# A transformer block on one core: the scale columns start from ones, one tile takes its scale from PSUM, the scale rows come in one block, the last transposes move ahead, and the second fc1 pass begins in other banks

## The chip, the cores and the metric

The kernel runs on one core of a Trainium2 chip. The core has five engines that each work through their own list of instructions in order: TensorE (PE, matrix products into the accumulator memory PSUM), VectorE (DVE), ScalarE (ACT), GpSimd (POOL) and SyncE (SP, which here only issues loads and stores). They wait for one another through semaphores. Transfers run on 16 DMA engines. PSUM has eight banks of 128 partitions by 512 float32 values. The metric is the device time of one execution in microseconds (us), the median of several runs.

## What is computed

A diffusion transformer block with modulation from a condition vector `c`, in bfloat16. There are B = 2 batches of N = 256 tokens, D = 1152 channels, F = 4608 hidden channels and two heads.

```python
mod = (_silu(c) @ w_mod).reshape(B, 6, 1, D)
shift_a, scale_a, gate_a, shift_m, scale_m, gate_m = [mod[:, i] for i in range(6)]
h = _layernorm(x, axis=-1) * (1 + scale_a) + shift_a
qkv = (h @ wqkv).reshape(B, N, 3, H, Dh)
...
attn = _softmax(jnp.einsum('bqhd,bkhd->bhqk', q, k) * Dh ** (-0.5), axis=-1)
a = jnp.einsum('bhqk,bkhd->bqhd', attn, v).reshape(B, N, D) @ wo
x = x + gate_a * a
h2 = _layernorm(x, axis=-1) * (1 + scale_m) + shift_m
m = _gelu(h2 @ w_fc1) @ w_fc2
return x + gate_m * m
```

The change touches the first layer norm with its scale `1 + scale_a`, the first projection that uses it (K), and the first product of the MLP (`h2 @ w_fc1`).

## The kernel before

**Planner.** The program text records every operation with its operands. A planner (class `Sched`) derives the dependencies and fixes each engine's order before anything runs. PE and SP keep the order in which the text records their work; DVE and ACT begin with the lists in `S.first` (L944) and then follow the planner's priorities; POOL follows the priorities. For PSUM the dependencies go by whole banks: an engine that reads a bank waits for the last matmul that PE wrote there, and PE waits for all readers before it writes the bank again. Nearly all matmuls are recorded by one helper line (L693) and the transposes on PE by another (L696), so in the profile they are told apart by form and by time.

**Tiles.** The 512 tokens are four tiles of 128: tiles 0 and 1 are batch 0, tiles 2 and 3 batch 1. The 1152 channels are nine groups of 128 (`KT = 9`); the first five (`KC = 5`) and the last four get their scale in two different ways.

**First layer norm** (L756). Tiles 1 and 3 take their statistics from DVE (L741, L742), tiles 0 and 2 from two ACT passes (L749, L750). POOL makes the reciprocal deviation (L745, L754). `xn_t` (L763, DVE) normalises the tile. `xn_T(t)` transposes it on PE in nine pieces into PSUM: for batch 0 into banks 4, 5 and 6, for batch 1 into 6, 4 and (group 8) 7.

**Scale, first five groups** (`sca`, `mod_kt`). Column-wise: for each group of the condition, five matmuls with two columns each add to ten columns of bank 7. The first one clears the bank. `sc1a` (L809, DVE) adds 1 and writes the ten columns to SBUF as `SC1A`. `hk` (L819 on DVE, L817 on ACT) multiplies a transposed piece by its column of `SC1A` and writes `HK`, the moving operand of the K product. `hk_0_0`, of group 0 and batch 0, reads the piece from SBUF; for the other four groups it is read from PSUM.

**K, first five groups** (L865). For batch 0, groups 0 to 4 are worked off one by one, each with four pairs of output columns (`k_pair`, two matmuls of 256 columns per pair). `xn_T(2)` stands behind group 1, `xn_T(3)` behind the first two pairs of group 4, then pairs 2 and 3 of group 4. The K product of batch 1 follows: `k_pair((0, 2, 1, 4, 3), 0, 1)`, which needs the five `hk` of batch 1.

**Scale, last four groups** (`scb`, L879). Row-wise: `quad_mm` makes for each of the nine groups of the condition four matmuls that use a quarter of the array each, into 32-partition stripes of bank 7. They stand in two blocks: condition groups 0 to 5, then six K matmuls of `k_pair((0, 2, 1), 1, 1)`, then condition groups 6 to 8. DVE then transposes the rows into columns (L888, `scb_T`), adds 1 (L890), and makes the `hk` of groups 5 to 8 (first of them `hk_5_0`), which K groups 5 to 8 need.

**Loads.** SP issues them in a fixed order from the start: x, the scale weights of the first five groups (in four pieces), K weights 0 to 4, the scale weights of the last four groups in three pieces of three condition groups each (`ld_sc5_0`, `ld_sc5_3`, `ld_sc5_6`), K weights 5 to 8, the shift weights, and then the Q weights, which overwrite the scale weights piece by piece and so wait for PE to have read them.

**MLP.** `xn2_T(t)` transposes the second norm's tiles 0 to 3 into PSUM (tile 2 into banks 7 and 6, tile 3 into banks 1 and 0: groups 0 to 3 in the first, 4 to 8 in the second). DVE (L1154) and ACT (L1157) scale and shift them into `H2T`. `fc1_tile(f, tok0, n)` (L1160) makes one 128-row piece of the hidden layer in one accumulator bank, which ACT empties with GELU (L1167). The accumulators rotate over the list `acc`: banks 2 to 5 at first. The first nine pieces (`F0 = 9`) are made for batch 0, then for batch 1; at that point (L1229) two banks are put at the front of the list:

```python
k = acc_rr[0] % 4
acc[:] = [0, 1] + acc[k:] + acc[:k]
```

So `fc1_0_256`, the first piece of batch 1, goes to bank 0 and `fc1_1_256` to bank 1. All later products take the six banks in turn.

Of the kernel before, what the change touches and what calls it, by code (L numbers as in the profile page):

```python
# [493 lines left out]
ALU = mybir.AluOpType  # L494
ACTF = mybir.ActivationFunctionType
# [5 lines left out]
KT = 9  # L501
# [8 lines left out]
KC = 5  # L510
# [5 lines left out]
def c_mm(n):  # L516
    return max(n / 2.4 + 2.5, 27.0)


def c_act(n, aps=0):  # L520
    return 190.0 + 0.8 * n + 75.0 * aps
# [10 lines left out]
def c_dve_fast(n):  # L532
    return 160.0 + 0.37 * n
# [10 lines left out]
def build_kernel(nc, x, c, wqkv, wo, w_mod, w_fc1, w_fc2, out):  # L544
    S = Sched()
# [4 lines left out]
    with (  # L550
# [4 lines left out]
        def sb(off, nbytes, dt=BF16):  # L555
            assert off % 4 == 0 and off + nbytes <= ARENA_BYTES, (off, nbytes)
            v = arena[:, off // 2:(off + nbytes) // 2]
            if dt == F32:
                v = v.bitcast(F32)
            return v  # L560

        def ps32(bank, c0=0, n=512):
            return psum[:, bank * 512 + c0: bank * 512 + c0 + n]

        def ps16(bank, c0=0, n=1024):
            v = psum[:, bank * 512: (bank + 1) * 512].bitcast(BF16)
            return v[:, c0:c0 + n]
# [15 lines left out]
        def misc(nbytes):  # L583
            o = mo[0]
            mo[0] += (nbytes + 3) // 4 * 4
            assert mo[0] <= ARENA_BYTES
            return o

        def wmat(o, f):
            return sb(o, KT * f * 2).rearrange("p (k f) -> p k f", k=KT)  # L590

        WSC = wmat(O_A, D)
# [41 lines left out]
        ONES = sb(misc(256), 256)  # L634
# [3 lines left out]
        ST = sb(misc(36), 36)  # L638
# [12 lines left out]
        NMR = sb(misc(16), 16, F32)  # L651
# [25 lines left out]
        def dve(cost, fn, reads, writes, name):  # L677
            return S.op("dve", cost, fn, reads=reads, writes=writes, name=name)

        def act(cost, fn, reads, writes, name):  # L680
            return S.op("act", cost, fn, reads=reads, writes=writes, name=name)
# [10 lines left out]
        def mm(o, l, r, st, sp, **kw):  # L692
            S.instr(lambda e: e.matmul(o, lhsT=l, rhs=r, start=st, stop=sp, **kw), reads=[l, r], writes=[o])  # L693
# [62 lines left out]
        for t in range(4):  # L756
            xt, xn, mv, rs = X[:, t, :], XN[:, t, :], MV[:, t, :], RSTD[:, t:t + 1]
            if t % 2 == 1:
                ln_stats_dve(xt, [X[:, t, i * CH:(i + 1) * CH] for i in range(NCH)], BN[:, t, :], mv, rs, "ln1_%d" % t)
            else:  # L760
                ln_stats_act(xt, xn, mv, SUMS[:, t:t + 1], rs, "ln1_%d" % t)
            m = MV[:, t, 0:1]
            dve(c_dve_fast(D), lambda e, xt=xt, xn=xn, m=m, rs=rs: e.tensor_scalar(out=xn, in0=xt, scalar1=m, scalar2=rs,  # L763
                                                                                 op0=ALU.subtract, op1=ALU.mult),
                [xt, m, rs], [xn], "xn_%d" % t)


        def xt_ps(b, kt, n=1):
            if b == 0:
                return (4, 5, 6)[kt // 4], (kt % 4) * 256  # L770
            return (7, 0) if kt == 8 else ((6, 4)[kt % 2], kt // 2 * 256)
# [8 lines left out]
        def xn_T_copy(b, kts, eng):  # L780
            bank, c0 = xt_ps(b, kts[0])
            n = len(kts)
            src = ps16(bank, c0, n * 256).rearrange("p (k t) -> p k t", k=n)
            st = kts[1] - kts[0] if n > 1 else 1
            copy_on(eng, HX[:, kts[0]:kts[-1] + 1:st, b * 256:(b + 1) * 256], src, n * 256, True, "xnT_cp%d_%d" % (b, kts[0]))

        def warm(n, tag):
            for i in range(n):
                S.unit("pe", 215.0, "warm_%s_%d" % (tag, i))
                mm(ps32(2), IDENT, Q4B, True, True)  # L790

        def mod_kt(W, kt, col0, name, fs=(0, 9)):
            S.unit("pe", (fs[1] - fs[0]) * 27.0, name)
            for f in range(*fs):
                mm(ps32(7, col0 + f * 2, 2), W[:, kt, f * 128:(f + 1) * 128], ST[:, kt:18:9], kt == 0 and f == fs[0], kt == KT - 1,
                   skip_group_check=True)

        def quads(w, g0, g1, q):
            return w.rearrange("p (g q c) -> p g q c", q=4, c=32)[:, g0:g1, q, :]

        def quad_mm(bank, w, g0, g1, kt):
            n = 32 * (g1 - g0)
            for q in range(4):
                o = psum[32 * q:32 * q + 2, bank * 512:bank * 512 + n].rearrange("p (g c) -> p g c", c=32)
                mm(o, ST[:, kt:18:9], quads(w, g0, g1, q), kt == 0, kt == KT - 1, tile_position=(0, 32 * q))

        def sc1a(ka, kb):
            m, o = ps32(7, 2 * ka, 2 * (kb - ka)), SC1A[:, 2 * ka:2 * kb]
            dve(170, lambda e: e.tensor_scalar(out=o, in0=m, scalar1=1.0, scalar2=None, op0=ALU.add), [m], [o], "sc1a_%d" % ka)  # L809


        def hk(kt, b, eng="dve"):
            dst, s1 = HK[:, kt, b * 256:(b + 1) * 256], SC1A[:, kt * 2 + b:kt * 2 + b + 1]
            bank, c0 = xt_ps(b, kt)
            src = ps16(bank, c0, 256) if kt < KC and kt + b > 0 else HX[:, kt, b * 256:(b + 1) * 256]
            if eng == "act":
                act(c_act(256, 1), lambda e: e.activation(out=dst, in_=src, func=ACTF.Copy, scale=s1), [src, s1], [dst], "hk_%d_%d" % (kt, b))  # L817
                return
            dve(256 if kt < KC else 200, lambda e: e.tensor_scalar(out=dst, in0=src, scalar1=s1, scalar2=None, op0=ALU.mult),  # L819
                [src, s1], [dst], "hk_%d_%d" % (kt, b))  # L820
# [10 lines left out]
        def k_pair(kts, i, b, bank=None):  # L831
            S.unit("pe", 2 * len(kts) * c_mm(256), "k%d_%d_%d" % (b, i, kts[0]))
            bank = KB[b][i] if bank is None else bank
            if kts[0] == 0:
                for kt in kts:
                    for half in range(2):
                        k_mm((kt,), 2 * i + half, b, bank, half)
            else:
                for half in range(2):
                    k_mm(kts, 2 * i + half, b, bank, half)  # L840
            if kts[-1] == KT - 1:
                eng = "act" if ev_rr[0] % 2 == 0 else "dve"
                ev_rr[0] += 1
                copy_on(eng, QK[:, 9 + 2 * i:11 + 2 * i, b * 256:(b + 1) * 256], ps32(bank).rearrange("p (j t) -> p j t", j=2), 512, False,
                        "k_ev%d_%d" % (b, i))

        warm(5, "b")
        for kt in range(0, 2):
            mod_kt(WSC, kt, 0, "sca_%d" % kt, (0, KC))
        warm(4, "c")  # L850
# [6 lines left out]
            mod_kt(WSC, kt, 0, "sca_%d" % kt, (0, KC))  # L857
        warm(1, "e")
        xn_T_copy(0, (0,), "dve")
        sc1a(0, KC)  # L860
        for kt in range(KC):
            hk(kt, 0, "act" if kt == 4 else "dve")
        xn_T_copy(0, (8,), "act")
        xn_T_copy(0, (5, 6, 7), "act")
        for kt in range(KC):  # L865
            for i in range(2 if kt == KC - 1 else 4):
                k_pair((kt,), i, 0)
            if kt == 1:
                xn_T(2)
        xn_T(3)  # L870
        k_pair((KC - 1,), 2, 0)
        k_pair((KC - 1,), 3, 0)
        xn_T_copy(1, (8,), "act")
        xn_T_copy(1, (5, 7), "act")
        xn_T_copy(1, (6,), "dve")
        for kt in range(KC):
            hk(kt, 1, "act" if kt % 2 else "dve")
        k_pair((0, 2, 1, 4, 3), 0, 1)
        S.unit("pe", 6 * 4 * 27.0, "scb_0")  # L879
        for kt in range(6):  # L880
            quad_mm(7, WSC[:, kt, :], KC, KT, kt)
        k_pair((0, 2, 1), 1, 1)
        S.unit("pe", 3 * 4 * 27.0, "scb_1")
        for kt in range(6, KT):
            quad_mm(7, WSC[:, kt, :], KC, KT, kt)
        n = 32 * (KT - KC)
        sct, scr = ps32(7, 0, n), MT[:, 0:n]
# [42 lines left out]
        for kt in range(KT):  # L930
            for b in range(2):
# [5 lines left out]
                else:  # L937
# [5 lines left out]

        S.first = {  # L944
# [5 lines left out]
        }  # L950

# [160 lines left out]
        acc = [2, 3, 4, 5]  # L1112
# [113 lines left out]
        dma(WFC2[:, 27:36, :], wfc2_v[:, 27:36, :], 9 * P * D * 2, "ld_wfc2_3", run=2304)  # L1226
        mlp_gate(last_h2T[0])
        k = acc_rr[0] % 4
        acc[:] = [0, 1] + acc[k:] + acc[:k]  # L1229
        acc_rr[0] = 0  # L1230
        for f in range(F0):
            fc1_tile(f, 256, 256)
# [8 lines left out]
        for t in range(4):  # L1241
            b = t // 2
# [3 lines left out]
            for (c0, c1) in pieces:  # L1246
                w = c1 - c0
                S.unit("pe", JT * c_mm(w), "fc2_%d_%d" % (t, c0))
                o = ps32(acc_bank(), 0, w)
# [62 lines left out]
```

## Time and profile before

| | |
|---|---|
| median of 3 runs | 244.43 us (244.30 to 244.53) |
| time of the profiled execution | 244.33 us |
| its span, first to last instruction | 242.6 us |
| PE busy | 237.5 us, 98% of the span |
| DVE, ACT, POOL busy | 116.2, 67.0, 22.4 us |
| granted TensorE clock | 1.00 |
| moved by DMA | 51.58 MB |

A line of the chain of waits reads: start in us, duration in us, engine, what it writes, source line, how many instructions. A line of a timeline reads: start, duration, engine, line, operation, output and input, form, count, and in brackets the idle time of the engine before it with what ended it. The weight loads of PE are listed as an engine of their own, PEld. A form such as `128*2` names the rows and columns of the array that are in use. Matmuls overlap, so one of 256 columns lasts 0.273 us in the profile while the next starts 0.109 us after it; the text calls these 0.109 its turn. The trace also holds the time of every semaphore mark; an operation's mark is what a waiting engine sees.

### The profile page before, as it was taken

Reading aid. Unit: us, or ns where it says so; the run is one execution under the profiler, and the core shown is the slowest. Engines: PE = TensorE matmul, PEld = TensorE weight load, DVE = VectorE, ACT = ScalarE, POOL = GpSimd, SP = SyncE. Lnnn points to the kernel's source line nnn. Section 1 sums busy time; section 2 is a strip of 40 time slices with the busy share of each in tenths; the row PEclk is TensorE's granted clock in tenths of the full one; section 3 lists DMA queues with packets and bytes.
Section 4 is the critical chain, followed back from the end, with each engine's and each line's share of the span. In section 5 each row is a group of like instructions: output and inputs, shape, how many; then the busy total and the mean of one; then the engine's idle time right before and its main releaser. Section 6 shows DMA issues by size and latency. Waiting matters only on the chain.

```text
span 242.6 us, 3964 instructions
## 1 busy us (share of the span) xinstructions
PE 237.5 (98%) x1700; PEld 145.0 (60%) x1700; DVE 116.2 (48%) x227; ACT 67.0 (28%) x138; POOL 22.4 (9%) x40
## 2 busy tenths in 40 slices
PE   7899999999999999999999999999999999999995
PEld 2588844466657656888644444444566566566564
DVE  2663447988983599669999600000022222111112
ACT  4820340436424206973233322222000000000000
POOL 1300000000023186400000110000000000000000
PEclk9999999999999999999999999999999999999999
DMA  6999999999996999969953499100000000000000
GB/s 220 378 372 390 391 387 385 404 415 406 389 353 195 357 393 392 392 188 399 351 165 83 163 317 369 44 0 3 0 16 19 16 16 16 19 16 16 21 28 19
DMA packets 30299, 51.58 MB, mean 213 GB/s; under 512 B 1611, under 2 KB 16971, under 8 KB 30283
## 3 DMA queue, kind: packets, MB, share of 16 engines
q1 hardware_dynamic: 29600, 50.14, 57.7%
q0 software_dynamic: 512, 1.19, 1.5%
q8 instruction: 13, 0.21, 0.4%
q10 hardware_dynamic: 171, 0.01, 0.0%
q14 instruction: 3, 0.02, 0.0%
HBM read 50.15 MB, written 1.19 MB: 212 GB/s over the span
## 4 chain that ended last, share of the span: by engine, by line
PE 95%; DMA 2%; ACT 1%; DVE 1%; issue 0%
PE psum L693 93%; PE psum L696 2%; DMA arena<-in_x_dram 2%; ACT arena L750 1%; ACT arena L749 0%; DVE arena L763 0%; DVE arena L819 0%; DVE arena L1254 0%; DVE arena L1255 0%; DVE arena L751 0%; DVE arena L809 0%; DVE arena L753 0%; ACT arena L733 0%
## 5 line engine op out<-in xcount | busy, mean ns | idle before, releaser
L693 PE MATMUL psum<-arena 128*128 128x384 bf16 (+8 forms) x1611 | 234.1, 314 | 2.2 <-POOL arena L719 1.5
L693 PEld LDWEIGHTS psum<-arena 128*128 128x128 bf16 (+2 forms) x1611 | 139.7, 97 | 92.2 <-issue 3.6
L1254 DVE TENSOR_TENSOR arena<-psum,arena 128x384 f32<-128x384 f32 (+2 forms) x13 | 6.8, 526 | 88.8 <-PE psum L693 88.8
L1167 ACT ACTIVATE arena<-psum 128x512 bf16<-128x512 f32 (+1 forms) x45 | 22.8, 511 | 42.4 <-PE psum L693 42.4
L688 ACT ACTIVATE arena<-psum 128x512 bf16<-128x512 f32 (+6 forms) x37 | 18.7, 534 | 36.2 <-PE psum L693 35.9
L1067 DVE SCALAR_TENSOR_TENSOR arena<-arena 128x1152 f32<-128x1152 bf16 x16 | 21.3, 1411 | 0.0
L1038 DVE SCALAR_TENSOR_TENSOR arena<-arena 128x896 f32<-128x896 bf16 x16 | 17.7, 1142 | 0.0
L690 DVE CAST arena<-psum 128x512 bf16<-128x512 f32 (+1 forms) x12 | 7.7, 646 | 10.0 <-PE psum L693 9.9
L674 POOL DMA_DIRECT2D dit_scratch<-arena x6 | 3.6, 605 | 92.9 <-ACT arena L688 53.6
L1133 POOL TENSOR_TENSOR arena<-arena 128x384 f32<-128x384 f32 x12 | 10.9, 911 | 10.7 <-DVE arena L1132 8.8
L741 DVE BATCH_NORM_STATS2 arena<-arena 128x6 f32<-128x384 f32 (+1 forms) x18 | 9.5, 549 | 4.2 <-DMA arena<-in_x_dram 3.5
L1138 ACT ACTIVATE arena<-arena 128x1152 bf16<-128x1152 f32 x4 | 5.4, 1344 | 9.7 <-DVE arena L1137 9.7
L1132 DVE TENSOR_TENSOR arena<-psum,arena 128x384 f32<-128x384 f32 x12 | 6.5, 546 | 2.8 <-DMA arena<-dit_scratch 2.0
L696 PE MATMUL psum<-arena 128*128 128x128 bf16 (+1 forms) x89 | 7.1, 219 | 0.4 <-DMA arena<-in_c_dram 0.3
L696 PEld LDWEIGHTS psum<-arena 128*128 128x128 bf16 (+1 forms) x89 | 5.8, 98 | 2.8 <-DMA arena<-in_c_dram 1.2
L1255 DVE TENSOR_TENSOR arena<-arena 128x384 bf16<-128x384 f32 (+2 forms) x13 | 6.9, 527 | 0.5
L1157 ACT ACTIVATE arena<-psum,arena 128x128 bf16<-128x128 bf16 x16 | 6.1, 455 | 2.9 <-PE psum L696 2.1
L1154 DVE TENSOR_SCALAR arena<-psum,arena 128x128 bf16<-128x128 bf16 x20 | 5.5, 335 | 2.9 <-PE psum L696 2.9
L982 ACT ACTIVATE arena<-psum,arena 128x256 bf16<-128x256 f32 x8 | 3.7, 469 | 0.4 <-DVE arena L979 0.3
L745 POOL TENSOR_TENSOR arena<-arena 128x1 f32<-128x1 f32 x6 | 3.3, 553 | 4.9 <-DVE arena L744 4.9
L935 ACT ACTIVATE arena<-arena 128x256 bf16<-128x256 bf16 x6 | 2.5, 495 | 3.3 <-DVE arena L929 3.3
L978 DVE TENSOR_REDUCE arena<-psum 128x2 f32<-128x512 f32 x4 | 2.7, 687 | 0.9 <-PE psum L693 0.9
(57 smaller groups left out, 52.5 us busy)
## 6 DMA issues: line engine op xcount, KB each, us to landing
arena<-in_w_fc_dram SPq DMA_DIRECT2D x9, 1152.0 KB, 6.9
arena<-in_w_fc_dram SPq DMA_DIRECT2D x4, 2592.0 KB, 18.2
arena<-in_w_mod_dram SPq DMA_DIRECT2D x3, 1920.0 KB, 19.6
arena<-in_wqkv_dram SPq DMA_DIRECT2D x18, 288.0 KB, 10.5
arena<-in_w_mod_dram SPq DMA_DIRECT2D x3, 864.0 KB, 13.2
arena<-in_wqkv_dram SPq DMA_DIRECT2D x1, 2592.0 KB, 16.7
arena<-in_wo_dram SPq DMA_DIRECT2D x1, 2592.0 KB, 26.1
arena<-in_w_mod_dram SPq DMA_DIRECT2D x1, 2592.0 KB, 17.6
```

What stands on the lines that cost most here:

```text
L688: act(c_act(n), lambda e: e.activation(out=dst, in_=src, func=ACTF.Copy), [src], [dst], name)
L690: dve(c_dve_psum16(n) if psum16 else c_dve_psum32(n), lambda e: e.tensor_copy(dst, src), [src], [dst], name)
L693: S.instr(lambda e: e.matmul(o, lhsT=l, rhs=r, start=st, stop=sp, **kw), reads=[l, r], writes=[o])
L696: S.instr(lambda e: e.transpose(o, i_, idn), reads=[i_, idn], writes=[o])
L741: dve(550, lambda e, s=s, o=o: e.bn_stats(out=o, in_=s), [s], [o], "bn_%s_%d" % (tag, ci))
L1038: dve(150 + FG * 1.1, lambda e, o=o, w=w, s1=s1: e.scalar_tensor_tensor(out=o, in0=w, scalar=s1, in1=o, op0=ALU.mult, op1=ALU.add), [w, s1 ...
L1067: u = dve(1300, lambda e, o=o, w=w, s1=s1: e.scalar_tensor_tensor(out=o, in0=w, scalar=s1, in1=o, op0=ALU.mult, op1=ALU.add), [w, s1, o], ...
L1132: dve(550, lambda e, o=o, ga=ga, x1c=x1c: e.tensor_tensor(out=x1c, in0=o, in1=ga, op=ALU.mult), [o, ga], [x1c], "wo_t1_%d_%d" % (t, ci))
L1133: S.op("pool", 930, lambda e, xs=xs, x1c=x1c: e.tensor_tensor(out=x1c, in0=x1c, in1=xs, op=ALU.add), reads=[x1c, xs], writes=[x1c], name=" ...
L1167: act(c_act(ntok), lambda e: e.activation(out=dst, in_=o, func=ACTF.Gelu_apprx_tanh), [o], [dst], "gelu_%d_%d" % (f, tok0))
L1254: dve(c_dve_psum32(w), lambda e, o=o, gm=gm, t1=t1: e.tensor_tensor(out=t1, in0=o, in1=gm, op=ALU.mult), [o, gm], [t1], "fc2_t1_%d_%d" % ( ...
L1255: dve(c_dve_32(w), lambda e, t1=t1, x1c=x1c, ost=ost: e.tensor_tensor(out=ost, in0=t1, in1=x1c, op=ALU.add), [t1, x1c], [ost], "fc2_out_%d ...
```

## The change

Six edits in one.

1. A new matmul `sca_one`, ahead of `sca_0`, multiplies ones by ones with one row each and writes 1 to the ten scale columns of bank 7. The `sca` matmuls all add to it, so the columns hold `1 + scale` when they are done. `sc1a` becomes a copy.
2. `hk_0_0` takes its scalar from column 0 of bank 7, not from `SC1A`. On DVE it moves ahead of `sc1a`.
3. `xn_2` becomes one ACT operation, scale times x plus bias, with the bias `-mean / deviation` from a new small DVE operation `nmr_2`. On DVE `xn_2` drops out of its place behind `hk_3_0`; on ACT it stands behind `xnT_cp0_5` and ahead of `hk_4_0`.
4. `xn_T(3)` stands behind one pair of K group 4, not two. Pairs 1 to 3 follow it.
5. The two blocks of scale rows become one, behind the six K matmuls that stood between them.
6. The two banks put at the front of the accumulators for the second fc1 pass are 6 and 7, not 0 and 1.

Beside these, the planner moves one accumulation step of the attention gate on DVE from behind the first softmax maximum to ahead of it. The orders of POOL and SP stay as they are.

```diff
@@ -760,6 +760,13 @@
             m = MV[:, t, 0:1]
+            if t == 2:
+                nm = NMR[:, t:t + 1]
+                dve(170, lambda e, nm=nm, m=m, rs=rs: e.scalar_tensor_tensor(out=nm, in0=m, scalar=-1.0, in1=rs, op0=ALU.mult, op1=ALU.mult),
+                    [m, rs], [nm], "nmr_%d" % t)
+                act(1344, lambda e, xt=xt, xn=xn, nm=nm, rs=rs: e.activation(out=xn, in_=xt, func=ACTF.Identity, scale=rs, bias=nm),
+                    [xt, rs, nm], [xn], "xn_%d" % t)
+                continue
@@ -792,7 +799,7 @@
-                mm(ps32(7, col0 + f * 2, 2), W[:, kt, f * 128:(f + 1) * 128], ST[:, kt:18:9], kt == 0 and f == fs[0], kt == KT - 1,
+                mm(ps32(7, col0 + f * 2, 2), W[:, kt, f * 128:(f + 1) * 128], ST[:, kt:18:9], False, kt == KT - 1,
@@ -806,11 +813,13 @@
-            dve(170, lambda e: e.tensor_scalar(out=o, in0=m, scalar1=1.0, scalar2=None, op0=ALU.add), [m], [o], "sc1a_%d" % ka)
+            dve(170, lambda e: e.tensor_copy(o, m), [m], [o], "sc1a_%d" % ka)
...
+            if kt + b == 0:
+                s1 = ps32(7, 0, 1)
@@ -845,6 +854,8 @@
         warm(5, "b")
+        S.unit("pe", 27.0, "sca_one")
+        mm(ps32(7, 0, 2 * KC), ONES[0:1, :], ONES[0:1, 0:2 * KC], True, False, skip_group_check=True)
@@ -857,31 +868,29 @@
         xn_T_copy(0, (0,), "dve")
+        hk(0, 0)
         sc1a(0, KC)
-        for kt in range(KC):
+        for kt in range(1, KC):
             hk(kt, 0, "act" if kt == 4 else "dve")
...
         for kt in range(KC):
-            for i in range(2 if kt == KC - 1 else 4):
+            for i in range(1 if kt == KC - 1 else 4):
                 k_pair((kt,), i, 0)
...
         xn_T(3)
-        k_pair((KC - 1,), 2, 0)
-        k_pair((KC - 1,), 3, 0)
+        for i in range(1, 4):
+            k_pair((KC - 1,), i, 0)
...
         k_pair((0, 2, 1, 4, 3), 0, 1)
-        S.unit("pe", 6 * 4 * 27.0, "scb_0")
-        for kt in range(6):
-            quad_mm(7, WSC[:, kt, :], KC, KT, kt)
         k_pair((0, 2, 1), 1, 1)
-        S.unit("pe", 3 * 4 * 27.0, "scb_1")
-        for kt in range(6, KT):
+        S.unit("pe", KT * 4 * 27.0, "scb")
+        for kt in range(KT):
             quad_mm(7, WSC[:, kt, :], KC, KT, kt)
@@ -943,9 +952,9 @@
-                    "xn_1", "xn_0", "nvar_ln1_2", "veps_ln1_2", "xnT_cp0_0", "sc1a_0", "hk_0_0", "hk_1_0", "hk_2_0", "hk_3_0", "xn_2",
+                    "xn_1", "xn_0", "nvar_ln1_2", "veps_ln1_2", "xnT_cp0_0", "nmr_2", "hk_0_0", "sc1a_0", "hk_1_0", "hk_2_0", "hk_3_0",
...
-            "act": ["touch", "ld_c", "sq_ln1_0", "c_tanh", "sum_ln1_0", "sq_ln1_2", "sum_ln1_2", "xnT_cp0_8", "xnT_cp0_5", "hk_4_0",
+            "act": ["touch", "ld_c", "sq_ln1_0", "c_tanh", "sum_ln1_0", "sq_ln1_2", "sum_ln1_2", "xnT_cp0_8", "xnT_cp0_5", "xn_2", "hk_4_0",
@@ -1226,7 +1235,7 @@
-        acc[:] = [0, 1] + acc[k:] + acc[:k]
+        acc[:] = [6, 7] + acc[k:] + acc[:k]
```

## The prediction

> **What bounds the kernel now.** I read the page first (part 1, busy shares; part 3, DMA queues), then the chain that ended last, the waits, and the timeline of single engines around each place that the diff touches. The PE row and two lines of the chain:
>
> ```profile
> PE 237.5 (98%) x1700; PEld 145.0 (60%) x1700; DVE 116.2 (48%) x227; ACT 67.0 (28%) x138; POOL 22.4 (9%) x40
> ...
> 17.12 41.75 PE psum L693 x333
> ...
> 108.42 131.75 PE psum L693 x792
> ```
>
> TensorE is the bound: from 17.12 us on, the chain is matmul behind matmul. So a gain must come from holes in PE's stream. There are four near the edits. Lines of the chain, then of the timelines of VectorE (DVE) and of the weight loads (PEld); in the brackets stands the idle time before and what ended it:
>
> ```profile
> 10.99 0.02 issue
> 11.02 0.18 DVE arena L809
> 11.20 0.02 issue
> 11.22 0.30 DVE arena L819
> 11.52 0.05 issue
> 11.57 1.92 PE psum L693 x16
> ...
> 108.35 0.06 issue
> ```
>
> ```profile
> 17.12 0.81 PEld L693 LDWEIGHTS psum<-arena 128*128 128x128 bf16 x8 [0.29 <-DVE arena L819]
> ...
> 18.36 0.99 PEld L693 LDWEIGHTS psum<-arena 128*2 128x2 bf16 x30 [0.21 <-issue]
> 19.55 0.71 PEld L693 LDWEIGHTS psum<-arena 128*2 128x2 bf16 x17 [0.21 <-DMA arena<-in_w_mod_dram]
> ...
> 20.19 0.32 DVE L888 STREAM_TRANSPOSE arena<-psum 128x128 f32<-128x128 f32 x1 [2.41 <-PE psum L693]
> ...
> 108.39 0.67 PEld L693 LDWEIGHTS psum<-arena 128*128 128x128 bf16 x7 [0.32 <-DVE arena L1154]
> ```
>
> In order: (1) PE idles until 11.57 while DVE adds 1 to the scale columns (L809) and then scales the first tile (L819). (2) At 17.12 it waits for the scaled tiles of batch 1. (3) The scale rows are made in two blocks of narrow matmuls (128*2 weight loads), at 18.36 and 19.55, with six K matmuls between. (4) At 108.4 the first second-half fc1 tile waits for the last normalised tile to leave its bank.
>
> One more view decides. The second scale-row block names a DMA as its releaser. That is `ld_sc5_6`, the last third of the scale-row weights, issued at 8.28; the view of its tile cut to that issue, and the DMA part of the page:
>
> ```profile
> L674 SPq DMA_DIRECT2D arena<-in_w_mod_dram x1: 1302/1302/1302, 8.3 to 8.3; - x1
> ...
> DMA to landing us min/median/max: 11.1/11.1/11.1
> ```
>
> ```profile
> DMA  6999999999996999969953499100000000000000
> ...
> q1 hardware_dynamic: 29600, 50.14, 57.7%
> ...
> q8 instruction: 13, 0.21, 0.4%
> ```
>
> 8.28 + 11.13 gives a landing at 19.41, only 0.145 us before the block's first matmul (19.556). The DMA engines are full from 6 to 70 us (nines), so a load in that stretch lands when its turn comes, whatever the compute engines do. Fifteen of that load's sixteen parts were in by 17.64; the sixteenth came at 19.41. The load before it (18.30 against 16.58) has the same late part, the one before that (15.65 against 15.50) has not. Between lies the first 16 KB packet of the instruction queue q8, at 15.33 for 1.14 us; PE had then started about 250 instructions, and at the next one (25.17) about 500.
>
> **The change part by part.** Against the profiled execution: span 242.60 us, time 244.33 (1.73 around the span), 0.10 under the median of 244.43.
>
> *Head.* L809 (0.17) leaves the path: today the last scale column is marked at 10.995, `sc1a` starts at 11.02, `hk_0_0` at 11.22. The 1 is put into PSUM by a ten-column matmul ahead of `sca_0`, and `hk_0_0` takes its scalar from PSUM, so it starts at 11.02: 0.205 us sooner, K matmuls at 11.36 instead of 11.567. A PSUM scalar has no row; the nearest are L819 from SBUF, 0.285, and from PSUM, 0.342; I take 0.285 and keep +0.06 as the other end. `sc1a`, now a copy, comes behind it (pitch 0.20) and `hk_1_0` still starts near 11.43, needed at 12.24. The ten-column matmul costs between 0.027 (a two-column row) and 0.25 (two changes of array form at 0.12, as around the transpose of c); PE idles 0.16 there for the first weights, so 0 to 0.1. The new `nmr_2` on DVE waits for POOL (10.69) and takes 0.16 to 0.77 (the rows of L1137): free up to 0.31, at worst 0.46 on `hk_0_0`; 0.16 is nearest, since the long rows had POOL working beside them and here POOL is done.
>
> *Tile 2 on ScalarE.* `xn_2` (0.57 on DVE) becomes one Identity on ACT, 1.16 (L750, same input) to 1.35 (L1138, same pointers). It starts at 10.97, ends by 12.3, and its transposes come at 13.12: free. Behind it ACT has `hk_4_0`, done near 12.8 instead of 11.7, needed at 15.37. DVE's chain to `xn_3` (three statistics, aggregate, POOL power) moves 0.49 forward: ready at 15.39 instead of 15.87.
>
> *Tile 3's transposes ahead.* They move past one K pair (2 x 0.109) and start at 15.59 instead of 16.01, 0.2 after `xn_3` is ready. The first scaled tile of batch 1 needs 1.11 us from there (17.122 - 16.010); PE now has 0.50 of transposes and six K matmuls, 0.66, together 1.16. The stall at 17.12 and the smaller one at 17.38 go: without them the tenth matmul from 16.949 on would start at 17.932, it starts at 18.155, so 0.22. POOL's and SP's orders stay as they are, so no transfer is issued in another order.
>
> *One scale-row block.* Each block costs an entry of 0.094 (18.358, where the matmul at 18.155 ends its turn of 0.109 at 18.264), an exit of 0.106 (18.798, where the last row group ends at 18.692) and 0.010 on the next matmul; one of two goes: 0.21.
>
> *What is late next.* These add up to 0.64 us, and PE would reach the last three row groups of the block at 18.92 instead of 19.556. They read the load that lands at 19.41. The six K matmuls that stood before them are now ahead of the whole block; nothing is queued that PE could do instead. They start at 19.41 + 0.047 (the restart seen at 6.739 behind a landing at 6.692) = 19.46. So 0.54 of the 0.64 becomes a DMA wait, and 0.10 is left. That wait is also the cover for everything above: each of the open prices (0.06, 0.1, 0.46, and even the loss of one whole item) only shortens it. Behind the block, K group 5 keeps its 0.32 of slack over `hk_5_0`, since DVE's transposition at L888 moves by the same 0.10. The first WQ load, which SP holds until the first row group is read, is issued 0.23 later, with ten microseconds of loads in the queues before it and 2.8 us of slack at its user.
>
> One rule speaks against the merged block. The 12 narrow matmuls at 19.56 mark their ends 34 ns apart (19.79 to 20.165), and L888 starts at 20.19 behind the last mark. The Trainium skill (TensorE: Matmul & The Clock Gate, section "The cost: per-tile semaphore tail") says that such increments serialize, with about 26 ns each; the trace agrees in kind, at 34 ns. With PE held until 19.46, the first 24 marks are out by 19.60 and the last 12 run from 19.69 to 20.07, so nothing changes in the sum; without the hold it caps the gain (rival A).
>
> *fc1 banks.* Today `fc1_0_256` writes bank 0, which holds groups 4 to 8 of the last tile until ACT's last L1157 ends (108.27); the trace shows it at 108.417 where the matmul before ends its turn at 108.189: 0.228. Banks 6 and 7 were emptied by 105.4, and the groups are needed one by one, the last at 109.06. So 0.228 goes, with no other wait in reach: after 109 us no load has less than 7 us of slack and GELU's evictions keep up.
>
> Sum: 0.098 + 0.228 = 0.33 us; 244.33 - 0.33 = 244.00 for that execution, 244.10 against the median.
>
> **The rivals.**
> A. *The load does not hold PE.* It needs the sixteenth part earlier than 18.87. For it: the lateness is one engine's, behind one instruction packet, and if that packet falls on another, the load is in between 18.5 and 19.2 (the other parts, 16.90 to 17.64, plus the 1.57 that C works out). Against: the packet belongs to PE's place in its program, which the change moves by one matmul and 0.2 to 0.3 us. The Trainium skill (Runtime: NRT & Kernel Launch, "Instruction fetch mechanics") states refills of 256 instructions in 16 KiB blocks over a queue of the engine's own, which fits the 13 packets here. Then the marks bind: a block starting at 18.58 marks 36 ends from 18.82 to 20.01, `hk_5_0` is ready 0.86 after L888 starts (20.04), at 20.90, and K group 5 starts at 20.94 instead of 21.367. Gain 0.42 + 0.23 = 0.65: 243.78.
> B. *The load lands a little later than in this trace*, at 19.51 or after in both kernels. The old one then waits as well, the K part gives nothing, 0.23 is left: 244.20.
> C. *Slower.* The load lands later in the changed kernel alone, because its instruction packet falls on the worst engine a second time. One such packet moved the sixteenth part by 1.57 (18.30 - 15.65 - 1.08, the step of the others). From a landing at 20.23 on (0.82 later) the time passes 244.92; at 1.57 it is 245.67. Against: packets are 250 PE instructions apart, the second at 25 us.
> D. *The moves at the head do nothing*, because `hk_0_0` or ACT is late: hidden by the hold, the time is the forecast's.
>
> **How the numbers follow.** Forecast (with D) 0.55; A, or part of it, 0.27; B 0.09; C, or something else that costs, 0.09. About 0.2% (0.49 us) is what a measurement of this kernel can tell from no change. Faster by more needs the load 0.16 earlier than in the trace: A and a part of the forecast's own spread, 0.33. Slower: 0.09. Within: 0.58. Range: 0.1 of spread among runs below A, 243.7, to no gain at all, 244.5; it leaves C out. The forecast's own range is 243.95 to 244.25.
>
> **What would show it.** `hk_0_0` (DVE) starting within 0.03 us of the last scale column's mark, K at about 11.36; no DVE wait of PE near 17; one run of narrow matmuls from about 18.6, with a wait of about 0.5 us inside it, ended by a DMA of w_mod near 19.4; L888's transposition at 20.1; no "issue" piece in the chain at 108. Wrong it would be if that load lands below 18.9 (then look at 20.9 for a wait on `hk_5_0`), if PE is held by something other than the load between 11 and 21 us, or if the six fc1 banks bring a wait later.

## The result

| | median (lowest to highest) | ratio to before, 95% interval |
|---|---|---|
| before | 244.44 us (244.30 to 244.75, 21 runs) | |
| changed kernel | 244.11 us (243.72 to 244.63, 21 runs) | 0.9986, 0.9980 to 0.9992 |
| changed kernel, second series | 243.97 us (243.78 to 244.18, 11 runs) | 0.9980, 0.9971 to 0.9989 |

The change is a small gain: 0.33 us in the first series, 0.46 us in the second (before: 244.43 there). Both are below the 0.49 us that the prediction called the least that can be told from no change, yet in both series the whole interval lies below 1. The forecast was 244.10, which is 0.01 below the first median and 0.13 above the second. The number was right; one of the steps that led to it was not.

### The profile after

The recorded execution took 243.98 us, with a span of 242.22 us; that of before had 244.33 and 242.60. The PE row of the page:

```profile
PE 237.1 (98%) x1701; PEld 145.1 (60%) x1701; DVE 115.8 (48%) x227; ACT 68.2 (28%) x139; POOL 22.4 (9%) x40
```

TensorE is still the bound. The chain that ended last, from 11 to 22 us (start, duration, engine, output, line, count):

```profile
11.08 0.03 issue
11.11 0.30 DVE arena L828
11.41 0.05 issue
11.46 1.92 PE psum L693 x16
...
16.50 3.80 PE psum L693 x64
20.30 0.32 DVE arena L897
...
20.64 0.18 DVE arena L899
...
20.85 0.30 DVE arena L828
21.14 0.05 issue
21.19 0.83 PE psum L693 x6
```

and around 108 us:

```profile
106.22 5.79 PE psum L693 x53
```

At the head only `hk_0_0` (now L828) stands between the last scale column and K; the addition is gone. At 108 no piece "issue" cuts the matmuls any more. But between 20.30 and 21.19 the chain has left PE: it goes through DVE's transposition of the scale rows (L897), the addition (L899) and `hk_5_0` (L828). The weight loads, and below them the timeline of DVE (in the brackets the idle time before and what ended it):

```profile
15.81 0.51 PEld L696 LDWEIGHTS psum<-arena 128*128 128x128 bf16 x9 [0.25 <-DVE arena L770]
16.28 2.34 PEld L693 LDWEIGHTS psum<-arena 128*128 128x128 bf16 x22
18.83 2.03 PEld L693 LDWEIGHTS psum<-arena 128*2 128x2 bf16 x50 [0.21 <-issue]
21.19 0.88 PEld L693 LDWEIGHTS psum<-arena 128*128 128x128 bf16 x9 [0.33 <-DVE arena L828]
```

```profile
12.58 1.48 DVE L741 BATCH_NORM_STATS2 arena<-arena 128x6 f32<-128x384 bf16 x3 [0.20 <-DMA arena<-in_x_dram]
...
15.18 0.58 DVE L770 TENSOR_SCALAR arena<-arena 128x1152 bf16<-128x1152 bf16 x1 [0.66 <-POOL arena L745]
...
20.29 0.32 DVE L897 STREAM_TRANSPOSE arena<-psum 128x128 f32<-128x128 f32 x1 [2.69 <-PE psum L693]
```

Three things are to be seen. The stall at 17 us is gone: 22 K matmuls in one run from 16.28. The narrow matmuls start at 18.83 and run through, with no DMA named; the last part of `ld_sc5_6` had landed at 18.645. And there are two new waits of PE: 0.25 (of which 0.14 is lost) at 15.81 for the normalised tile 3 (L770), whose statistics (L741) had waited 0.20 for the load of x, and 0.33 (0.21 lost) at 21.19 for `hk_5_0`. The marks show where the second one comes from: the last of the 36 narrow matmuls starts at 19.29, but their marks run from 19.07 to 20.26, 34 ns apart, and DVE's transposition starts 0.024 behind the last of them.

| | before | after | difference |
|---|---|---|---|
| K starts | 11.567 | 11.455 | -0.112 |
| transposes of tile 3 | 16.010 | 15.820 | -0.190 |
| first narrow matmul | 18.358 | 18.834 | (six K matmuls later) |
| DVE's transposition | 20.189 | 20.286 | +0.097 |
| K group 5 | 21.367 | 21.191 | -0.176 |
| just before the second fc1 pass begins | | | -0.164 |
| just behind its first pieces | | | -0.388 |

So the fc1 banks gave 0.224 and all the rest 0.164.

### The profile page after: what moved, and what is told of

The parts are those of the page before. It is cut to its first block, busy times and chain, and to the rows that moved or that the text cites. A ratio compares the mean times of both kernels' runs of the same rounds, so it can differ in the third digit from the quotient of the medians.

```text
span 242.2 us, 3967 instructions
## 1 busy us (share of the span) xinstructions
PE 237.1 (98%) x1701; PEld 145.1 (60%) x1701; DVE 115.8 (48%) x227; ACT 68.2 (28%) x139; POOL 22.4 (9%) x40
## 4 chain that ended last, share of the span: by engine, by line
PE 95%; DMA 2%; DVE 1%; ACT 1%; issue 0%
PE psum L693 93%; PE psum L696 2%; DMA arena<-in_x_dram 2%; ACT arena L750 1%; ACT arena L749 0%; DVE arena L828 0%; DVE arena L770 0%; DVE arena L897 0%; DVE arena L1263 0%; DVE arena L1264 0%; DVE arena L751 0%; DVE arena L899 0%; DVE arena L753 0%; ACT arena L733 0%
## 5 line engine op out<-in xcount | busy, mean ns | idle before, releaser
L693 PE MATMUL psum<-arena 128*128 128x384 bf16 (+8 forms) x1612 | 233.6, 313 | 2.1 <-POOL arena L719 1.5
L693 PEld LDWEIGHTS psum<-arena 128*128 128x128 bf16 (+2 forms) x1612 | 139.9, 97 | 91.4 <-issue 3.3
L741 DVE BATCH_NORM_STATS2 arena<-arena 128x6 f32<-128x384 f32 (+1 forms) x18 | 9.5, 550 | 4.4 <-DMA arena<-in_x_dram 3.7
L1163 DVE TENSOR_SCALAR arena<-psum,arena 128x128 bf16<-128x128 bf16 x20 | 5.5, 337 | 2.9 <-PE psum L696 2.9
```

What stands on the lines that cost most here:

```text
L741: dve(550, lambda e, s=s, o=o: e.bn_stats(out=o, in_=s), [s], [o], "bn_%s_%d" % (tag, ci))
```

## The experiments

Two theories stood at the start. **Load**: the forecast's; PE is held by `ld_sc5_6` in the usual execution, and this covers the other edits. **Marks**: rival A's mechanism; the load is in time, and K group 5 waits for `hk_5_0`, which stands behind 36 marks that PE writes one after the other.

### The fc1 banks alone, and everything but them

```diff
# kernel before
-        acc[:] = [0, 1] + acc[k:] + acc[:k]
+        acc[:] = [6, 7] + acc[k:] + acc[:k]
```

> The kernel before with edit 6 alone (banks 6 and 7 at the front of the accumulators). Both theories: the piece at 108 us loses its 0.228 us of waiting for ScalarE and nothing takes its place, so 0.23 us less than before, 244.21 when before is at 244.44. If the changed kernel's whole gain of 0.33 came with the banks, this kernel would reach 244.11.

Measured: 244.18 (244.11 to 245.45), before 244.44; ratio 0.9993 (0.9977 to 1.0009). That interval, widened by two runs above 245, includes no change, so it is the trace that shows the gain. The weight loads of the two kernels around 108 us, first the banks alone, then the changed kernel with the old banks:

```profile
107.46 2.61 PEld L693 LDWEIGHTS psum<-arena 128*128 128x128 bf16 x24
```

```diff
# changed kernel
-        acc[:] = [6, 7] + acc[k:] + acc[:k]
+        acc[:] = [0, 1] + acc[k:] + acc[:k]
```

> The changed kernel with edit 6 undone (banks 0 and 1 again): what is left is edits 1 to 5. Theory 1, the forecast's (the last third of the scale-row weights holds TensorE until about 19.4 in the usual execution): 0.10 us less than before, 244.34, with a wait of about 0.5 us inside the narrow matmuls, ended by a transfer of w_mod. Theory 2 (that load is in time, and K group 5 is held by hk_5_0, which stands behind 36 serial marks and DVE's transposition): 0.17 us less, 244.27, with a wait of 0.2 us at 21 ended by DVE. In both the 0.23 us at 108 is back.

Measured: 244.20 (244.00 to 244.46), ratio 0.9986 (0.9973 to 0.9998).

```profile
107.50 0.32 PEld L693 LDWEIGHTS psum<-arena 128*128 128x128 bf16 x3
108.14 2.42 PEld L693 LDWEIGHTS psum<-arena 128*128 128x128 bf16 x23 [0.32 <-DVE arena L1163]
```

The wait comes and goes with the banks: of the fourteen traces, the five with banks 0 and 1 have it and the nine with 6 and 7 have not. (The view names DVE as its end; L1163 here is L1154 of the kernel before. In the trace of before the mark that comes last is ScalarE's, L1157, at 108.28.) The medians put the banks at 0.26 and edits 1 to 5 at 0.24, against 0.228 and 0.10 (load) or 0.17 (marks). Their sum, 0.50, is above the 0.33 and the 0.46 of the whole change; differences of this size between series are not resolved here. In the trace with the old banks the narrow matmuls ran through, the load had landed at 18.76, and K group 5 waited for `hk_5_0` at 21.10. That speaks for the marks.

### One mark instead of 36

```diff
# changed kernel, where the planner numbers and writes PE's marks
+                    elif u.name == "scb" and ins is not u.instrs[-1]:
+                        ins.eidx = eidx[e] + 1
...
-                    else:
+                    elif u.name != "scb" or ins is u.instrs[-1]:
                         bi.then_inc(sems[e], 1)
```

> The changed kernel, but of the 36 narrow matmuls of the scale rows only the last one adds to TensorE's semaphore; everything that waits for any of them waits for that. Theory 1: TensorE is held by the load, so the marks do not matter: 244.1, no change against the changed kernel. Theory 2: DVE's transposition starts about 0.5 us earlier (19.75 instead of 20.29), the wait of 0.21 us at K group 5 goes, and the time is 243.89, 0.55 less than before.

Measured: 243.80 (243.51 to 245.41), ratio 0.9980 (0.9962 to 0.9998): what the marks theory said, within 0.1. But its recorded execution (243.99, above its median) shows the wait that the load theory described. Weight loads, then DVE (this edit adds two lines to the text, so that L695 here is L693 of the changed kernel and L899 is its L897, the transposition):

```profile
18.55 0.32 PEld L695 LDWEIGHTS psum<-arena 128*2 128x2 bf16 x24 [0.21 <-issue]
19.39 2.24 PEld L695 LDWEIGHTS psum<-arena 128*2 128x2 bf16 x31 [0.52 <-DMA arena<-in_w_mod_dram]
```

```profile
19.79 0.32 DVE L899 STREAM_TRANSPOSE arena<-psum 128x128 f32<-128x128 f32 x1 [2.46 <-PE psum L695]
```

Here the load landed at 19.352, and PE lost 0.50 us inside the block. DVE's transposition still comes 0.50 us earlier than in the changed kernel, 0.39 behind the first matmul after the hold, and K group 5 no longer waits for DVE. So both mechanisms exist, and the load's landing differs between the traces so far by up to 0.8 us. That this is a difference of executions and not of kernels is seen best in the kernel with the banks alone: up to 108 us it is the kernel before, and yet the load landed at 18.81 there and at 19.41 in the trace of before.

### Two blocks, as before

```diff
# changed kernel
+        S.unit("pe", 6 * 4 * 27.0, "scb_0")
+        for kt in range(6):
+            quad_mm(7, WSC[:, kt, :], KC, KT, kt)
         k_pair((0, 2, 1), 1, 1)
-        S.unit("pe", KT * 4 * 27.0, "scb")
-        for kt in range(KT):
+        S.unit("pe", 3 * 4 * 27.0, "scb_1")
+        for kt in range(6, KT):
```

> The changed kernel with edit 5 undone: the scale rows in two blocks with six K matmuls between them, as before. Theory 1: the load holds both arrangements, 244.1 to 244.15. Theory 2: the second block starts about 19.2, when 24 of the 36 marks are long out; DVE's transposition starts at about 19.9, K group 5 no longer waits, but the second entry and exit cost 0.21 us on TensorE, so K group 5 starts at 21.18 as in the changed kernel: 244.11, no change. If joining the blocks had given its 0.21 us, this kernel would take 244.32.

Measured: 243.88 (243.79 to 244.54), ratio 0.9975 (0.9963 to 0.9988). Weight loads:

```profile
18.12 0.99 PEld L693 LDWEIGHTS psum<-arena 128*2 128x2 bf16 x30 [0.21 <-issue]
19.32 2.68 PEld L693 LDWEIGHTS psum<-arena 128*2 128x2 bf16 x35 [0.21 <-DMA arena<-in_w_mod_dram]
```

The second entry is back (two times 0.21 idle), and no wait at 21. From K's start to K group 5 this trace takes 9.585 us; the kernel with the old banks, one block and neither the load nor tile 3 late, takes 9.586 (21.103 - 11.517). In these two traces joining the blocks is worth nothing: what PE saves at the second entry, K group 5 waits for `hk_5_0`. Why the median lies 0.09 to 0.23 below the two of the changed kernel is not settled; the intervals of the ratios overlap.

### Joining the blocks in the kernel before

```diff
# kernel before
-        S.unit("pe", 6 * 4 * 27.0, "scb_0")
-        for kt in range(6):
-            quad_mm(7, WSC[:, kt, :], KC, KT, kt)
         k_pair((0, 2, 1), 1, 1)
-        S.unit("pe", 3 * 4 * 27.0, "scb_1")
-        for kt in range(6, KT):
+        S.unit("pe", KT * 4 * 27.0, "scb")
+        for kt in range(KT):
```

> The kernel before with edit 5 alone. The forecast's term, 0.21 saved where nothing else holds TensorE: 244.22. Marks: the block starts at 19.01, K group 5 comes 2.36 later, at 21.37, which is where it is today: 244.43, no gain, and hk_5_0 now ends the wait. A load at 19.41 would hold the last third by 0.1 us, hidden behind the marks.

Measured: 244.47 (244.33 to 245.47), before 244.46; ratio 1.0001 (0.9990 to 1.0012).

```profile
18.97 2.03 PEld L693 LDWEIGHTS psum<-arena 128*2 128x2 bf16 x50 [0.21 <-issue]
21.32 0.33 PEld L693 LDWEIGHTS psum<-arena 128*128 128x128 bf16 x4 [0.32 <-DVE arena L819]
```

No gain, and a wait for `hk_5_0` where there was none, as the marks theory said. The forecast's term of 0.21 does not appear. The load (19.13) was in before PE reached it (19.26).

### The changed kernel again, and its load made later

The second series of the changed kernel ran beside the next three.

> The changed kernel once more, beside the next three. The sixteenth part of the last scale-row load landed at 19.41 and 19.35 in two executions (the kernel before; the one with one mark), at 18.65 and 18.76 in two others (the changed kernel; the one with the old fc1 banks). Theory 1, the hold is usual: median 244.1, and an execution with the landing near 19.4 shows a wait on w_mod inside the narrow matmuls. Theory 2, the marks bind: median 244.0 to 244.1, landing below 19.0 and a wait on hk_5_0 near 21.1.

Measured: 243.97 (243.78 to 244.18). The recorded execution took 243.79; its weight loads:

```profile
18.65 2.03 PEld L693 LDWEIGHTS psum<-arena 128*2 128x2 bf16 x50 [0.21 <-issue]
21.00 0.66 PEld L693 LDWEIGHTS psum<-arena 128*128 128x128 bf16 x7 [0.32 <-DVE arena L828]
```

The load landed at 18.70, nothing is held, K group 5 waits 0.21 for `hk_5_0`. Three of the eleven runs lie at 243.78 to 243.81: rival A's 243.78.

```diff
# changed kernel, order of SP's loads
-  ... ld_sc5_3, ld_sc5_6, ld_wk5, ld_wk6 ...
+  ... ld_sc5_3, ld_wk5, ld_sc5_6, ld_wk6 ...
```

> The changed kernel with the load of the last third of the scale-row weights issued behind that of K group 5, so that it lands 0.75 us later. In the runs so far K group 5 starts 1.85 us after a landing that holds TensorE, and at 21.19 where none does. Theory 1 (usual landing 19.41, already holding): landing 20.16, K group 5 at 22.01, 0.74 later than with the hold: 244.85. Theory 2 (usual landing 18.65): landing 19.40, K group 5 at 21.25, 0.06 later than in the changed kernel: 244.15.

Measured: 244.46 (244.02 to 244.72), 0.49 above the changed kernel in the same series: between the two expectations (0.06 and 0.74). Its recorded execution, at 244.46 too, is late for another reason. DVE, then weight loads (L743, L772 and L830 here are L741, L770 and L828 of the changed kernel):

```profile
13.07 1.48 DVE L743 BATCH_NORM_STATS2 arena<-arena 128x6 f32<-128x384 bf16 x3 [0.33 <-DMA arena<-in_x_dram]
```

```profile
16.30 0.51 PEld L696 LDWEIGHTS psum<-arena 128*128 128x128 bf16 x9 [0.38 <-DVE arena L772]
...
19.32 2.03 PEld L693 LDWEIGHTS psum<-arena 128*2 128x2 bf16 x50 [0.21 <-issue]
21.67 0.33 PEld L693 LDWEIGHTS psum<-arena 128*128 128x128 bf16 x4 [0.32 <-DVE arena L830]
```

The load landed at 19.58, just ahead of its use at 19.61, because tile 3 of x had been late (13.05) and pushed PE back. So no trace shows the later load holding PE: the 0.49 of the median fits a load that is partly felt, but that the load costs it is not shown. In how many executions the load holds the changed kernel stays open; in the three traces with its K part unaltered (changed, changed again, old fc1 banks) it did not.

### The block out of reach of the load: one mark, and 36

```diff
# changed kernel; with the one-mark edit above, and without it
         k_pair((0, 2, 1), 1, 1)
+        k_pair((4, 3), 1, 1)
         S.unit("pe", KT * 4 * 27.0, "scb")
...
-        k_pair((4, 3), 1, 1)
         k_pair((0, 2, 1, 4, 3), 2, 1)
```

> The changed kernel with one mark for the 36 narrow matmuls and the block four K matmuls later: by its place it starts at 19.27 and needs the last load at 19.52, later than any landing seen, and DVE's transposition starts about 19.9, so that hk_5_0 (20.8) is in time for K group 5 (20.97). Neither load nor marks can hold it, by both theories: 0.22 below the changed kernel's profiled 243.98, so 243.76, and 243.65 to 243.8 with a narrower spread (runs of the kernel with one mark alone lie from 243.5 to 244.0 beside two far off). If neither load nor marks mattered for the spread of 0.9 us in the changed kernel's times, the spread stays.

Measured: 243.68 (five of six runs from 243.58 to 243.81, one at 245.38), ratio 0.9982 (0.9959 to 1.0005; the one high run makes the interval wide). K group 5 waits for nothing in its trace.

> The changed kernel with the block four K matmuls later, as in the run before last, but with all 36 marks. The load can't hold it there. Marks theory: in the second trace of the changed kernel K group 5 starts 2.36 us after the block; the block moves 0.44 later, so K group 5 goes from 21.00 to 21.44 and waits 0.65 us on hk_5_0: 243.79 + 0.44 = 244.23, up to 244.35 with the spread of the start, 0.55 to 0.65 above the same kernel with one mark (243.68). Load theory: the load alone made the spread, so this kernel is as fast as the one with one mark, 243.7.

Measured: 244.34 (244.20 to 246.52), ratio 1.0008 (0.9990 to 1.0025).

```profile
19.87 1.59 PEld L693 LDWEIGHTS psum<-arena 128*2 128x2 bf16 x46 [0.21 <-issue]
22.22 0.77 PEld L693 LDWEIGHTS psum<-arena 128*128 128x128 bf16 x8 [0.76 <-DVE arena L828]
```

The two kernels differ in the marks alone. With 36 of them the whole gain of the change is lost: 0.66 between the medians of the two series, about as expected (0.55 to 0.65). The intervals of the two ratios overlap, since each kernel has one or more runs far above its median; it is the trace that settles the marks. PE loses 0.645 there waiting for `hk_5_0`, and K group 5 starts 2.355 behind the block, as in the changed kernel, although four K matmuls fewer stand between. The version with one mark is the fastest of all here, 0.29 below the changed kernel of the same series and 0.75 below before, but on six runs.

### One mark per block in the kernel before

```diff
# kernel before
+                    elif u.name in ("scb_0", "scb_1") and ins is not u.instrs[-1]:
+                        ins.eidx = eidx[e] + 1
...
-                    else:
+                    elif u.name not in ("scb_0", "scb_1") or ins is u.instrs[-1]:
                         bi.then_inc(sems[e], 1)
```

> The kernel before, its two blocks with one mark each. Marks theory: the marks cost TensorE nothing, only the one who waits for the last of them; K group 5 has 0.32 us of slack over hk_5_0, so no change, 244.43, while DVE's transposition at L888 starts about 0.25 earlier. If a mark also cost time on TensorE itself, 0.03 us each, the time would fall.

Measured: 244.42 (244.33 to 244.57), before 244.46: no change, though DVE's transposition starts 0.39 behind the second block instead of 0.63. 34 marks fewer at 0.03 each would have been 1 us of PE's time. The marks cost the one who waits for the last of them, not PE.

### The head alone, and all but tiles 2 and 3

```diff
# kernel before; edits 1 and 2 as in the change
+        mm(ps32(7, 0, 2 * KC), ONES[0:1, :], ONES[0:1, 0:2 * KC], True, False, skip_group_check=True)
...
+            if kt + b == 0:
+                s1 = ps32(7, 0, 1)
...
+        hk(0, 0)
         sc1a(0, KC)
-        for kt in range(KC):
+        for kt in range(1, KC):
```

> The kernel before with edits 1 and 2 alone. K starts 0.11 to 0.2 us earlier. The transposes of tile 3, today at 16.01 with the tile ready at 15.87 and seen 0.05 later, can move by 0.09 only; the stall for the scaled tiles of batch 1 stays. Both theories: 0.09 us less, 244.35. If the head's 0.2 us came through whole: 244.24. If sca_one costs what the head saves: 244.44.

Measured: 244.33 (244.28 to 244.66), before 244.43; ratio 0.9990 (0.9978 to 1.0003). Weight loads at the transposes of tile 3:

```profile
15.98 0.51 PEld L696 LDWEIGHTS psum<-arena 128*128 128x128 bf16 x9 [0.15 <-DVE arena L763]
```

Between the medians 0.10 of the head's 0.2 comes through. The trace shows where the rest goes: K starts 0.136 behind the mark of `hk_0_0` instead of 0.046 (see the last section), which takes 0.09, and the transposes then wait 0.03 for `xn_3` (L763). Without the first loss the second would have been 0.12, so `xn_3` sets the limit, as expected. The other way round:

```diff
# changed kernel, edits 3 and 4 undone
-            if t == 2:
-                ... nmr_2, xn_2 on ACT ...
-                continue
...
-            for i in range(1 if kt == KC - 1 else 4):
+            for i in range(2 if kt == KC - 1 else 4):
```

> The changed kernel with edits 3 and 4 undone (tile 2 normalised on DVE, the transposes of tile 3 behind two K pairs). Marks theory: the transposes of tile 3 start at 15.98 as in the run with the head alone, the stall near 17.1 stays, the block starts at 19.00, K group 5 at 21.36, as before; what is left is the fc1 banks: 244.20, that is 0.1 to 0.2 above the changed kernel. Load theory: the hold covers edits 3 and 4, so no change against the changed kernel, 244.0 to 244.1.

Measured: 244.23 (244.05 to 245.73), ratio 0.9995 (0.9982 to 1.0007). Weight loads:

```profile
16.21 0.51 PEld L696 LDWEIGHTS psum<-arena 128*128 128x128 bf16 x9 [0.35 <-DVE arena L763]
...
17.34 1.68 PEld L693 LDWEIGHTS psum<-arena 128*128 128x128 bf16 x16 [0.29 <-DVE arena L821]
19.23 2.03 PEld L693 LDWEIGHTS psum<-arena 128*2 128x2 bf16 x50 [0.21 <-issue]
21.58 0.44 PEld L693 LDWEIGHTS psum<-arena 128*128 128x128 bf16 x5 [0.33 <-DVE arena L821]
```

The stall at 17 is back (L821 here is L819 of the kernel before), and the median is 0.12 to 0.26 above those of the changed kernel. The intervals of the ratios overlap, and K starts 0.09 later here as with the head alone, so this is a rough size for edits 3 and 4; in the trace no hold covers their loss.

### What the traces show together

Every trace with one block and 36 marks, in us:

| kernel | tile 3 of x landed | `xn_3` marked | its transposes | block starts | `ld_sc5_6` landed | K group 5 |
|---|---|---|---|---|---|---|
| changed | 12.556 | 15.773 | 15.820 | 18.834 | 18.645 | 21.191 |
| changed, again | 12.370 | 15.590 | 15.635 | 18.648 | 18.699 | 21.004 |
| old fc1 banks | 12.277 | 15.540 | 15.741 | 18.744 | 18.764 | 21.103 |
| load later | 13.046 | 16.262 | 16.308 | 19.321 | 19.581 | 21.678 |
| tiles as before | 12.955 | 16.169 | 16.215 | 19.229 | 19.025 | 21.585 |
| block later | 13.156 | 16.375 | 16.421 | 19.871 | 19.067 | 22.226 |
| joined only | 12.461 | 15.828 | 15.966 | 18.969 | 19.128 | 21.325 |

K group 5 minus the start of the block is 2.355 to 2.359 in all seven, whatever the load does. And where DVE stood waiting for tile 3 of x, the mark of `xn_3` follows the landing of that tile by 3.214 to 3.220 us (the first two rows, load later, tiles as before, block later; also 3.218 with the banks alone, 3.218 with one mark, 3.216 with one mark and the block later). So the wait at 15.8 is a wait for a load, and how late that load is differs by a microsecond between executions (12.12 to 13.20 over all fourteen traces). This would fit the wider spread of the changed kernel's times in the first series, 0.91 us against 0.45 before. No experiment moved that load; this second limit is read from the traces alone.

## Why the number was right and a step was not

**The step that failed is "What is late next".** It said that PE reaches the last three row groups at 18.92 and starts them at 19.46, behind the load. In the four traces of kernels with edits 1 to 5 (changed, changed again, old fc1 banks, one mark) the load landed at 18.645, 18.70, 18.76 and 19.35, and to lose nothing PE needed it at 19.12, 18.94, 19.03 and 18.85 (0.29 behind the block's start): only the last one was held. The landing of 19.41 was taken for a property of the queue order. It is one draw: over the thirteen traces with the loads in their old order it lies between 18.53 and 19.41. In its place stand the marks. They put K group 5 2.36 behind the block's first matmul, 0.21 more than the matmuls need (0.608 for the block and 1.538 for the 14 K matmuls behind it make 2.146).

**Rival A's mechanism is what happened**, its time only in the best executions. It put K group 5 at 20.94 from a block at 18.58, which is the measured 2.36. In the recorded execution the block starts 0.25 later than A had it: 0.10 because K starts at 11.455 and not at 11.36, and most of the rest, 0.14, because tile 3 is waited for. Rivals B and C needed a landing after 19.41; none of the thirteen traces has one.

**Why the number held all the same.** The load and the marks are limits that lie close together. K group 5 starts 1.85 behind a landing that holds PE (read from the one-mark trace), so a landing at 19.41 would put it at 21.265; the marks and the late tile put it at 21.19. The forecast gave the K part 0.10; PE's matmuls behind K group 5 come 0.166 earlier in the trace. That the two limits lie so close in this execution is luck, and so is the number: in the second trace K group 5 starts at 21.00.

Point by point:

- *Head.* From the last scale column's mark to K: 0.572 before, 0.375 after, so 0.197 for the forecast's 0.205. The PSUM scalar costs 0.293 instead of 0.285, `nmr_2` its 0.16, and `hk_0_0` starts 0.025 behind the mark. `sca_one` costs nothing that shows. Everything ahead came 0.085 later in this execution (x landed at 4.70 instead of 4.62), which leaves 0.112.
- *Tile 2 on ScalarE.* The price was right (1.347, bounds 1.16 and 1.35) and free. The term that was mis-sized is `xn_3` "0.49 forward": 0.10 in the recorded trace, 0.28 in the second. The forecast counted DVE's time and did not ask for the next input: tile 3 of x, landing at 12.27 before, had 0.42 us of cover behind `hk_3_0` and `xn_2`. Without them DVE stood waiting there, 0.20 in the recorded trace.
- *Tile 3's transposes ahead.* The stall at 17.12 is gone as predicted. Undoing edits 3 and 4 costs 0.12 to 0.26 between medians.
- *One block.* PE does save 0.21 of entry and exit, but K group 5 waits 0.21 for the marks. Alone the edit gives 244.47 against 244.46.
- *fc1 banks.* 0.228 forecast, 0.224 in the trace, 0.26 between medians.
- *The prices called open because the hold covers them.* In the traces of the changed kernel there was no cover. The head came through in part, and undoing edits 3 and 4 was felt.

One paragraph of the prediction spoke against the merged block: the Trainium skill (TensorE: Matmul & The Clock Gate, section "The cost: per-tile semaphore tail") says that increments serialize and that a single one on the last tile suffices. The runs agree in kind, though the skill's figure is about 26 ns for one increment and the marks here come 34 ns apart; one mark for 36 is worth 0.17 to 0.31 in place (243.80 against the two medians) and 0.66 where the marks fully show.

## What to carry to other kernels

Count the marks as well as the instructions: here PE began the last of 36 short matmuls at 19.29 and its mark came at 20.26, and whoever waits for the last mark pays; where nobody needs the marks between, a single one on the last matmul saves that time. When an edit takes work out of the way of a wait, look for the next input of the engine that is freed, its load's landing above all, and compare it with the new time and not with the old. A landing read from one trace is one draw: if two limits lie within a few tenths, a forecast should carry both.

## What the runs showed that was not expected

- The last of `ld_sc5_6`'s sixteen parts came 1.77 us behind the fifteenth in the trace of before, 0.54 and 0.79 in the two of the changed kernel, 0.34 to 1.54 in the others with the same order of loads. The prediction laid this to a packet of the instruction queue; no run tried that. The traces lean that way without deciding it: where the first 16 KB packet began before 15.55 (before, one mark, two blocks) the part was 1.5 to 1.8 late, where it began after 16.2 (tiles as before, block later, banks alone) 0.3 to 0.5; but with one mark per block in the kernel before it began at 15.86 and the part was 1.50 late as well.
- In the kernels with the head alone and with the tiles as before, K starts 0.136 us behind the mark of `hk_0_0`, in all others with the new head 0.045 to 0.047. What differs in the traces is that the first matmul lists DVE's semaphore ahead of that of a load which had landed 0.81 and 0.21 us before that mark. Whether this order is the cause was not tried.
- A trace can lie far from its kernel's median: with the block later 245.01 against 244.34, with the banks alone 244.58 against 244.18; in both tile 3 of x landed after 13.1.
